# q and k of one chunk of tokens by seven block products instead of eight, and the gate's logits as two columns of v's products

## The chip, the cores and the metric

The kernel runs on one core of one Trainium2 chip. The time is the device time in microseconds, here the median of 3 timed runs; beside it stands one profiled execution, from which all rows below come. TensorE multiplies matrices and accumulates in PSUM (8 banks of 128 partitions x 512 float32), VectorE, ScalarE and GpSimd work element by element, and SyncE issues the DMAs.

## The reference

```python
x = A_x                                     # 2048 tokens x 448
g = sigmoid((x * gate_w).sum(-1))           # one gate per token
qkv = x @ wqkv                              # 16 heads of 28
logits = q . k over 8 past positions, 2 apart, * 28**-0.5
o = softmax(logits) . v                     # the same 8 positions
a = o @ wo
h = relu(x @ w1 + b1) ** 2                  # 1792 wide
b = h @ w2 + b2
out = g * a + (1 - g) * b
```

All products are wanted in float32 accuracy.

## The kernel before, in words

Tokens come in four chunks of 512 (chunk c holds four tiles of 128 tokens). Each float32 operand is split into a high part, rounded to the TensorE type (`fp32r`), and a low part, the rest; a product is made of three passes, high by high, high by low and low by high. ScalarE makes the high part (a copy), VectorE the low part (a subtraction): `split_full`. The 448 rows over which q, k and v are summed are three whole row tiles of 128 and a last one of 64. So that 64 rows do not take the time of 128, nearly all products are made of 64 rows at a time, two of them side by side in the two halves of the array (`side_by_side`), into two different banks; when the halves of a bank's sum change sides, a small VectorE write to the bank (`turn`) orders the one after the other.

`qkv_first` makes q, k and v of the first chunk (36 whole products of 128 rows, then pairs), `qkv_two` those of the others, two token tiles at a time. `qkv_evacuate` copies a finished bank to a stage tile with ScalarE; SyncE stores stage tiles to q_d, k_d and v_d in DRAM, from which attention (GpSimd multiplies, VectorE reduces) loads them again with its neighbours. Attention's first loads are issued when the second chunk's stores are, and wait for them.

The gate's logits are computed by VectorE from the raw chunk (`z_product`, `z_sums`), stored, loaded in another order and summed (`z_store`, `z_load`, `z_last`).

The program is written by one pass over TensorE's work that keeps a clock of its own (`advance`); `when(t, ...)` puts a step of another engine at a time of that clock, which sets only the place in each engine's queue, in which it then waits for its data. Steps of that kind are the splits of each chunk's x (`SPLIT_AT`), the spilling of x to DRAM for the MLP, and the four quarters of w1 (`w1_piece(i, t, gap)`: the load where it is called, the splits from t on). Raw loads of x, w1 and w2 share two buffers (`rawp`).

After the four chunks come the MLP (banks h, then b) and the products with wo (banks a), in an order written out by hand.

Of the kernel before, what the change touches and what calls it, by code (L numbers as in the profile page):

```python
# [14 lines left out]
P = 128  # L15
# [8 lines left out]
NQ = D + 2  # L24
NZ = 64
NP = 512
# [31 lines left out]
def gated_mix_kernel(ctx: ExitStack, tc: tile.TileContext, xT, wqkv, w1, w2, wo, b1, b2, out):  # L58
# [11 lines left out]
    z_d = tc.dram_tile([P, NZ], F32, name="z_d")  # L70
# [10 lines left out]
    w1h = const.tile([P, 3, F], F32R, name="w1h")  # L81
    w1l = const.tile([P, 3, F], F32R, name="w1l")
# [8 lines left out]

    xpool = ctx.enter_context(tc.tile_pool(name="xpool", bufs=1))
# [5 lines left out]
    zg = smallp.tile([P, 6, NS], F32, name="zg")  # L98
    zt, gt, g1t = zg[:, 0:2], zg[:, 2:4], zg[:, 4:6]
# [54 lines left out]
    wqh = ap.tile([P, 3, NP + 2 * D], F32R, name="wqh")  # L154
    wql = ap.tile([P, 3, NP + 2 * D], F32R, name="wql")

    w7h = ap.tile([P, NP + D], F32R, name="w7h")
    w7l = ap.tile([P, NP + D], F32R, name="w7l")
# [3 lines left out]
    nc.gpsimd.memset(halo0, 0.0)  # L162

    stage = {}

    def block(b):

        o = (0, NP, NP + D)[b]
        return slice(o, o + D)
# [29 lines left out]
    def qkv_evacuate(pt, c, tl, b):  # L199
        par, t = c // 2, (c % 2) * 4 + tl  # L200
        first = (b, t // 2) not in stage
        if first:
            stage[b, t // 2] = xap.tile([P, G, 2, C], F32, tag="stage", name=f"st{c}_{tl}_{b}", bufs=ST_BUFS)
        st = stage[b, t // 2]
        nc.scalar.activation(st[:, :, t % 2], pt[:, :D].rearrange("p (g c) -> p g c", g=G), AF.Copy)  # L205
        if not first:
            stage.pop((b, t // 2))
            t0 = t - t % 2
            dst, off = ((q_d, 0), (k_d, HALO), (v_d, HALO))[b]
            dd = dst[par, :, off:off + SP].rearrange("g (p s) c -> p g s c", s=NS)[:, :, t0:t0 + 2]  # L210
            nc.sync.dma_start(dd.rearrange("p g s c -> p g (s c)"), st.rearrange("p g s c -> p g (s c)"))
# [9 lines left out]
    def last(x, acc, tl, b):  # L221

        sl = slice(tl * P, tl * P + P)
        n = block(1) if b == 2 else slice(0, D)
        h, l = w7h[:, n], w7l[:, n]
        return [(acc, x.x7[:, sl], h), (acc, x.x7[:, sl], l), (acc, x.x8[:, sl], h)]

    def accs(c, b, tls, tags):
        return [Acc(t, f"qkv{c}_{tl}_{b}", D) for t, tl in zip(tags, tls)]
# [60 lines left out]


# [101 lines left out]
    def gates(par):  # L393

        e = smp.tile([P, 32], F32, tag="e", name=f"e{par}")[:, :NS]
        nc.scalar.activation(e, zt[:, par], AF.Exp, scale=-1.0)
# [127 lines left out]
    def w1_piece(i, dt, gap):  # L524
# [4 lines left out]
        sl = slice(i * n, (i + 1) * n)  # L529

        def part(k):
            if k < 3 and i > 1:
                split_copied(dt + k * gap, raw[:, k, :n], [(slice(0, P), slice(0, n), w1h[:, k, sl], w1l[:, k, sl])])
                return
            if k < 3:
                split_full(raw[:, k, :n], w1h[:, k, sl], w1l[:, k, sl], soon)
                return
# [47 lines left out]
    def h_full(x, acc, f, ks):  # L585
        fs = slice(f * P, f * P + P)
        return sum((three(acc, w1h[:, k, fs], w1l[:, k, fs], x.h[k], x.l[k]) for k in ks), [])
# [11 lines left out]
    def h_turn(accs, f):  # L599
        touch(w1h[:, 2].rearrange("p (f n) -> p f n", n=P)[:, f:f + 2, 0:1])  # L600
        for a in accs:
            a.rows = None
# [34 lines left out]
    raws = [raw_tile("wqraw0")]  # L637
    rx = raw_tile("xraw0")
    for k in range(4):
        if k < 3:  # L640
            nc.sync.dma_start(raws[0][:, k, :NQ], wqkv[0, :, k])
        else:
            for b, rows in ((0, slice(0, 64)), (1, slice(64, P))):
                nc.sync.dma_start(raws[0][rows, k, :NQ], wqkv[b, rows, k])
# [3 lines left out]
    for b, tag in ((1, "k"), (2, "v")):  # L648
        raw = attp.tile([P, 3, D], F32, tag=tag, name=f"wqraw{b}")
        for k in range(3):  # L650
            nc.sync.dma_start(raw[:, k], wqkv[b, :, k, :D])
        raws.append(raw)
    raw7 = attp.tile([P, D], F32, tag="q", name="wqraw7")
    nc.sync.dma_start(raw7, wqkv[2, :, 3, :D])
    x = x_tiles(0, xap)
    for k in range(3):
        nc.scalar.activation(wqh[:, k, :D], raws[0][:, k, :D], AF.Copy)
# [7 lines left out]
        nc.vector.tensor_sub(wql[:, k, :D], raws[0][:, k, :D], f32(wqh[:, k, :D]))  # L665
        for cols in halves:
            nc.vector.tensor_sub(x.l[k][:, cols], rx[:, k, cols], f32(x.h[k][:, cols]))
    split_full(raws[0][:, 3, :D], w7h[:, :D], w7l[:, :D])
    split_x78(rx[:, 3], x.x7, x.x8)

    zs = smp.tile([P, 3, NZ], F32, tag="lg", name="zs")
    zu = xcp.tile([P, CH], F32, tag="zu", name="zu")
    zpart, zall, gw = zs[:, 0], zs[:, 1], zs[:, 2, 0:4]
    nc.vector.tensor_copy(gw, raws[0][:, :, D])

    def z_product(raw, k):

        r = slice(0, P if k < 3 else 64)
        if k:
            nc.vector.scalar_tensor_tensor(zu[r], raw[r, k], gw[r, k:k + 1], zu[r], op0=ALU.mult, op1=ALU.add)  # L680
        else:
            nc.vector.tensor_scalar_mul(zu, raw[:, 0], gw[:, 0:1])

    def z_sums(c):

        nc.vector.transpose(zu, zu)
        nc.vector.tensor_reduce(
            zpart.rearrange("p (b c t) -> p c t b", b=4, c=4)[:, c],
            zu.rearrange("p (t b r) -> p t b r", t=4, b=4), axis=AX.X, op=ALU.add)

    def z_store():

        nc.sync.dma_start(z_d, zpart)

    def z_load():

        for b in range(4):
            nc.sync.dma_start(
                zall[b * 32:b * 32 + 32].rearrange("p (a n) -> p a n", a=4),
                z_d[:, b * 16:b * 16 + 16].rearrange("(a c) n -> c a n", a=4))  # L700

    def z_last():

        nc.vector.tensor_reduce(
            zt.rearrange("p q s -> p (q s)"), zall.rearrange("p (a n) -> p n a", a=4), axis=AX.X, op=ALU.add)

    def wq_split(b, k):
        if k < 3:
            split_full(raws[b][:, k], wqh[:, k, block(b)], wql[:, k, block(b)])
        else:  # L710
            split_full(raw7, w7h[:, NP:], w7l[:, NP:])
# [8 lines left out]
    SPLIT_AT = {1: 19000.0, 2: 35000.0, 3: 53500.0}  # L720

    def x_begin(c):
# [6 lines left out]
        if c == 1:  # L729
            xs[c] = X(own, [prodp.tile([P, W * C], F32R, tag="pp", name=f"x{c}_3{n}", bufs=PP_BUFS)[:, 48:48 + CH]  # L730
                            for n in range(2)])
            return
        xm[c] = x_tiles(c, xpool)
        xs[c] = X(own + xm[c].t[3:])
        for j in range(3):
            at(12000.0 + j * 2000.0, lambda j=j: nc.scalar.activation(xm[c].t[j], f32(own[j]), AF.Copy))
# [16 lines left out]
    for k in range(4):  # L753
        when(15000.0 + k * 700.0, z_product, rx, k)
    when(17900.0, z_sums, 0)
    when(60500.0, z_store)
    when(76000.0, z_load)
    when(86500.0, z_last)
    for c, t in SPLIT_AT.items():
        when(t, x_begin, c)  # L760
        for k in range(4):
            when(t + k * 900.0, lambda c, k: x_split(xraw[c], xs[c], k), c, k)
            when(t + k * 900.0 + 450.0, lambda c, k: z_product(xraw[c], k), c, k)
        when(t + 4200.0, z_sums, c)
# [456 lines left out]
```

## Time and profile before

| what | value |
|---|---|
| timed runs, median (lowest to highest) | 413.44 us (413.13 to 413.84) |
| profiled execution, first to last instruction | 412.0 us |
| TensorE busy | 407.8 us (99%) |
| VectorE, ScalarE, GpSimd busy | 270.6, 210.4, 268.4 us |
| DMA, mean over the span | 73.83 MB, 179 GB/s |

The profiled execution is given by its span; the timed runs' median lies 1.4 us above it, for what comes before the first and after the last instruction. Rows of the trace give start and duration in us, engine, line, operation, destination<-sources and shape; in brackets stands how long the engine had been idle and what ended that. "64*128" is a product of 64 rows in one half of the array, "128*128" one of all 128 rows. PEld is the loading of weights, which runs beside the products.

### The profile page before, as it was taken

How to read it: one execution, taken by the hardware profiler on the slowest of the kernel's cores; microseconds unless marked ns; L12 is line 12 of the kernel's file. 1: busy time of each engine (PE TensorE's matmuls, PEld its weight loads, DVE VectorE, ACT ScalarE, POOL GpSimd, SP SyncE). 2: the span in 40 equal slices, each digit the busy share in tenths (PEclk: the TensorE clock that was granted, in tenths of full speed). 3: DMA queues.
4: the chain of work that ended last, by engine and by line, in shares of the span. 5: the costliest groups of instructions: out<-in, count | busy, mean ns of one | idle time of the engine just before them, and what ended most of it. 6: DMA issues, size and time to landing. Idle time of an engine off the chain costs nothing.

```text
span 412.0 us, 9331 instructions
## 1 busy us (share of the span) xinstructions
PE 407.8 (99%) x3835; PEld 366.0 (89%) x3835; DVE 270.6 (66%) x430; ACT 210.4 (51%) x461; POOL 268.4 (65%) x167
## 2 busy tenths in 40 slices
PE   8999999999999999999999999999999999999997
PEld 7999999999888888888888888989898888888996
DVE  4590745276767766787656798879576677892354
ACT  4641646387775555444565535444653254346540
POOL 0000001955999999989989899999899977940000
PEclk9999999999999999999999999999999999999999
DMA  7999999979262315654112649765146530168304
GB/s 213 368 351 309 286 390 288 355 223 315 91 241 99 128 51 209 208 186 152 41 47 105 222 158 270 196 146 154 28 157 200 217 130 2 45 179 132 95 0 181
DMA packets 66763, 73.83 MB, mean 179 GB/s; under 512 B 33120, under 2 KB 59296, under 8 KB 66464
## 3 DMA queue, kind: packets, MB, share of 16 engines
q1 hardware_dynamic: 66720, 73.23, 55.4%
q8 instruction: 30, 0.49, 0.5%
q14 instruction: 13, 0.11, 0.1%
HBM read 45.74 MB, written 28.28 MB: 180 GB/s over the span
## 4 chain that ended last, share of the span: by engine, by line
PE 99%; DVE 0%; issue 0%
PE b L186 33%; PE h L186 32%; PE qkv L186 23%; PE a L186 7%; PE qkv L255 2%; PE warm L634 1%; PE a L993 1%; PE last L993 0%; DVE bt L872 0%; PE last L985 0%; PE a L985 0%; DVE zero L631 0%; DVE b1z L632 0%
## 5 line engine op out<-in xcount | busy, mean ns | idle before, releaser
L335 POOL TENSOR_TENSOR qk<-q,k 128x896 f32<-128x896 f32 x64 | 135.2, 2144 | 84.2 <-DMA k<-k_d 76.0
L342 POOL TENSOR_TENSOR av<-lg,v 128x896 f32<-128x896 f32 x64 | 119.2, 1957 | 6.2 <-DVE lg L336 5.6
L621 DVE TENSOR_TENSOR h<-h,h 128x512 fp32r<-128x512 f32 x56 | 38.4, 688 | 66.8 <-ACT h L624 66.5
L186 PE MATMUL qkv<-wqh,x 64*128 64x448 f32 x528 | 78.2, 359 | 0.0
L336 DVE TENSOR_REDUCE lg<-qk 128x32 f32<-128x896 f32 x64 | 67.0, 1074 | 0.0
L350 DVE TENSOR_REDUCE o<-av 128x112 f32<-128x896 f32 x64 | 66.4, 1070 | 0.1
L186 PE MATMUL b<-w2ah,h 64*128 64x448 f32 x448 | 66.3, 359 | 0.0
L186 PE MATMUL b<-w2bh,h 64*128 64x448 f32 x448 | 66.1, 359 | 0.0
L622 ACT ACTIVATE h<-h,b1z 128x512 f32<-128x512 f32 x56 | 36.7, 655 | 43.6 <-PE h L186 43.6
L186 PEld LDWEIGHTS qkv<-wqh,x 64*128 64x128 f32 x528 | 49.4, 184 | 3.6
L186 PE MATMUL qkv<-wql,x 64*128 64x448 f32 x264 | 47.7, 358 | 0.0
L186 PEld LDWEIGHTS b<-w2bh,h 64*128 64x128 f32 x448 | 42.1, 184 | 3.5
L186 PEld LDWEIGHTS b<-w2ah,h 64*128 64x128 f32 x448 | 42.0, 184 | 3.7
L205 ACT ACTIVATE st<-qkv 128x448 f32<-128x448 f32 x48 | 23.5, 542 | 34.3 <-PE qkv L186 31.7
L186 PE MATMUL b<-w2bl,h 64*128 64x448 f32 x224 | 40.7, 358 | 0.0
L186 PE MATMUL b<-w2al,h 64*128 64x448 f32 x224 | 40.5, 358 | 0.0
L623 ACT ACTIVATE h<-h 128x512 fp32r<-128x512 f32 x56 | 33.5, 598 | 1.7
L624 ACT ACTIVATE h<-h 128x512 f32<-128x512 f32 x56 | 33.3, 594 | 0.0
L573 ACT ACTIVATE h<-h 128x4 fp32r<-128x4 f32 (+1 forms) x35 | 7.2, 207 | 44.4 <-PE b L186 44.2
L186 PE MATMUL h<-x2b,w1h 64*128 64x512 f32 x168 | 28.1, 386 | 0.0
L186 PE MATMUL h<-x,w1h 64*128 64x512 f32 x168 | 28.1, 386 | 0.0
L186 PE MATMUL h<-x1b,w1h 64*128 64x512 f32 x168 | 28.1, 386 | 0.0
(150 smaller groups left out, 688.6 us busy)
## 6 DMA issues: line engine op xcount, KB each, us to landing
k<-k_d SPq DMA_DIRECT2D x8, 840.0 KB, 5.6
v<-v_d SPq DMA_DIRECT2D x8, 840.0 KB, 5.0
x_d<-x SPq DMA_DIRECT2D x11, 512.0 KB, 6.8
q_d<-st SPq DMA_DIRECT2D x8, 448.0 KB, 5.5
k_d<-st SPq DMA_DIRECT2D x8, 448.0 KB, 5.2
v_d<-st SPq DMA_DIRECT2D x8, 448.0 KB, 5.8
w1raw<-w SPq DMA_DIRECT2D x4, 896.0 KB, 9.2
q<-q_d SPq DMA_DIRECT2D x8, 448.0 KB, 3.6
```

The source lines that it names most:

```text
L186: nc.tensor.matmul(acc.pt[:, :acc.n], a[rows], w[rows], start=acc.todo == acc.all, stop=acc.todo == 1)
L205: nc.scalar.activation(st[:, :, t % 2], pt[:, :D].rearrange("p (g c) -> p g c", g=G), AF.Copy)
L255: nc.tensor.matmul(acc.pt[:, :D], a, w, start=k == j == 0, stop=False)
L335: nc.gpsimd.tensor_mul(pr, q[:, s:s + 1].to_broadcast([P, W, C]), k[:, s:s + W])
L336: pending.append(lambda: nc.vector.tensor_reduce(lg[:, s], pr.rearrange("p w (h d) -> p w h d", h=HG), axis=AX.X, op=ALU.add))
L342: nc.gpsimd.tensor_mul(pr.rearrange("p (h d) w -> p w h d", h=HG), lg[:, s][:, :, :, None].to_broadcast([P, W, HG, DH]), v[:, s:s + W].rea ...
L350: nc.vector.tensor_reduce(o[:, g * C:(g + 1) * C], pr, axis=AX.X, op=ALU.add)
L573: nc.scalar.activation(ap, f32(ap), AF.Copy)
L621: nc.vector.tensor_sub(hl, pt, f32(hh))
L622: ops += [lambda pt=pt, r=r: nc.scalar.activation(pt, pt, AF.Relu, bias=b1t[:, f + r:f + r + 1]), lambda pt=pt, hh=hh: nc.scalar.activatio ...
L623: lambda pt=pt, hh=hh: nc.scalar.activation(hh, pt, AF.Square),
L624: lambda pt=pt, r=r, low=low: (nc.scalar.activation(pt, pt, AF.Square), at(delays[r], low))]
```

## The change

Of the third chunk (c = 2), the four tiles are two groups of two. Within a group, two token tiles by two row tiles times two row tiles by two outputs (q and k) is a product of 2 by 2 blocks; it is made of seven block products of sums of blocks (Strassen's way, in Winograd's form) instead of eight. The row tiles 0 and 1 are one such product of whole tiles; the last tile of 64 rows with half of tile 2 is another, on half of the rows (`part`), the two groups side by side. The other half of tile 2 is done in the old way (`rest`). Sums of weights are made in the raw tiles and split (`weight_sums`, into the not yet used places of w2), sums of tokens in the raw chunk (`token_sums`). The seven products are added up in four banks per group, x, y, z and w: products 1, 6 and 7 in x, with a copy of x by ScalarE to a stage tile after each (`copied`), after which the next goes on adding; banks y, w, z and x are then added to the stage tiles by VectorE (`added`). v of this chunk comes first, by whole products (`v_tiles`).

The gate's weights are two more columns (450 instead of 448) of v's weights in all chunks, and ScalarE copies one of them with each v.

To fit, w1 is held in two halves, and steps move: x of the fourth chunk is loaded at 47500 of the clock instead of 39500, the second quarter of w1 at 54000 instead of 46500 with its splits from 60500 instead of 58500, and the copies of the fourth chunk's x for the MLP (`x_copies`) come after the third chunk.

```diff
     def block(b):
-        o = (0, NP, NP + D)[b]
-        return slice(o, o + D)
+        return slice(b * D, b * D + (NV if b == 2 else D))
...
+        if b == 2:
+            nc.scalar.activation(zt[par][:, t:t + 1], pt[:, D:D + 1], AF.Copy)
...
+    class Bank:
...
+            nc.tensor.matmul(self.pt[:, :self.n], a, w, start=new, stop=True, skip_group_check=True)
...
+    def whole(*todo):
+        for bank, prods in todo:
+            for a, w in prods:
+                bank.add(a, w)
+            advance(3 * MM448)
+
+    def halved(low, high):
+        for two in zip(low[1], high[1]):
+            for bank, (a, w) in zip((low[0], high[0]), two):
+                bank.add(a, w)
+        advance(3 * MM448)
...
+            one, two = (2, 3) if half else (0, 1)
+            return {1: lambda: (self.tokens(0, one), q(one)), 2: lambda: (self.tokens(0, two), q(two)),
+                    3: lambda: (self.token_sums(4, two), k(two)), 4: lambda: (self.tokens(1, two), wsum[4, half]),
+                    5: lambda: (self.token_sums(1, two), wsum[1, half]),
+                    6: lambda: (self.token_sums(2, one), wsum[2, half]),
+                    7: lambda: (self.token_sums(3, one), wsum[3, half])}[n]()
...
+            name = {1: "x", 2: "y", 3: "z", 4: "w", 5: "z", 6: "x", 7: "x"}[n]
...
+        def copied(self, n, b, r):
+            nc.scalar.activation(self.stage(b)[:, :, r], heads(self.to(n).pt), AF.Copy)
+
+        def added(self, n, b, r, store=False):
+            st = self.stage(b)
+            nc.vector.tensor_add(st[:, :, r], heads(self.to(n).pt), st[:, :, r])
...
+        parts(1)
+        parts(2)
+        turned(2)
+        wholes(1)
+        each("copied", 1, 0, 0)
+        wholes(2)
+        other(2, 0, 0)
+        each("added", 2, 0, 0)
+        parts(5)
+        wholes(5)
+        each("copied", 5, 1, 1)
+        parts(4)
+        turned(4)
+        parts(6)
+        wholes(6)
+        each("copied", 6, 1, 0)
+        wholes(4)
+        other(4, 1, 0)
+        other(3, 0, 1)
+        turned(3)
+        parts(7)
+        wholes(7)
+        each("copied", 7, 0, 1)
+        each("added", 4, 0, 1, True)
+        wholes(3)
+        parts(3)
+        each("added", 3, 1, 0)
+        other(7, 1, 1)
+        each("added", 7, 1, 1, True)
+
+    def v_tiles(c, x, tls, inner):
+        two = [(Bank(f"v{c}_{tl}", "b", NV), tl) for tl in tls]
...
+        for bank, tl in two:
+            whole(*((bank, ops(tl, j)) for j in range(3)))
+        halved(*((bank, [(a[rows], w[rows]) for a, w in ops(tl, 3)]) for (bank, tl), rows in zip(two, (LOW, HIGH))))
+        for bank, tl in two:
+            qkv_evacuate(bank.pt, c, tl, 2, inner)
...
+    nc.sync.dma_start(raw7[:, 0], wqkv[2, :, 3])
+    for b, rows in ((1, slice(0, 64)), (0, slice(64, P))):
+        nc.sync.dma_start(raw7[rows, 1, :D], wqkv[b, rows, 3, :D])
...
-    SPLIT_AT = {1: 19000.0, 2: 35000.0, 3: 53500.0}
+    SPLIT_AT = {1: 19000.0, 2: 35000.0, 3: 55000.0}
...
-    when(17900.0, z_sums, 0)
-    when(60500.0, z_store)
-    when(76000.0, z_load)
-    when(86500.0, z_last)
+    steps(24000.0, 900.0, weight_sums())
...
-            when(t + 4500.0, x_more, c + 1)
...
+    when(23500.0, x_more, 2)
+    when(47500.0, x_more, 3)
+    when(46900.0, lambda: steps(47000.0, 900.0, token_sums(2)))
...
-    when(46500.0, w1_piece, 1, 58500.0, 1500.0)
-    when(67000.0, w1_piece, 2, 77400.0, 1450.0)
...
+    when(54000.0, w1_piece, 1, 60500.0, 1500.0)
+    when(66000.0, w1_piece, 2, 75600.0, 1450.0)
...
+    v_tiles(2, xs[2], (0, 1), True)
+    v_tiles(2, xs[2], (2, 3), True)
+    qk_seven(2, xs[2])
+    x_copies(3)
```

In SyncE's queue, around the end of the second chunk, before (w1raw_795 is the second quarter of w1; st, the stage tiles of the second chunk's last q, k and v; q, k and v, attention's first loads):

```order
L528 DMA w1raw_795<-w 128x4x448 [waits DMAHW0_49,DVE_49]
L211 DMA q_d<-st_2_0_809 128x4x224 [waits DMAHW1_49,Activation_49]
L211 DMA k_d<-st_3_1_811 128x4x224 [waits DMAHW2_49,Activation_49]
L211 DMA v_d<-st_2_2_853 128x4x224 [waits DMAHW3_49,Activation_49]
L306 DMA q_857<-q_d 128x896 [waits DMAHW4_49,DMAHW1_49]
L307 DMA k_858<-k_d 128x1680 [waits DMAHW6_49,DMAHW5_49,DMAHW2_49]
L312 DMA v_861<-v_d 128x1680 [waits DMAHW7_49,DMAHW3_49]
```

The same place now (xraw_833 is x of the fourth chunk, w1raw_927 the second quarter of w1):

```order
L772 DMA xraw_833<-xT 128x2048 [waits DMAHW0_49,DVE_49]
L225 DMA q_d<-st_2_0_835 128x4x224 [waits DMAHW1_49,Activation_49]
L225 DMA k_d<-st_3_1_837 128x4x224 [waits DMAHW2_49,Activation_49]
L225 DMA v_d<-st_2_2_892 128x4x224 [waits DMAHW3_49,Activation_49]
L507 DMA q_898<-q_d 128x896 [waits DMAHW4_49,DMAHW1_49]
L508 DMA k_899<-k_d 128x1680 [waits DMAHW6_49,DMAHW5_49,DMAHW2_49]
L513 DMA v_902<-v_d 128x1680 [waits DMAHW7_49,DMAHW3_49]
L729 DMA w1raw_927<-w 128x4x448 [waits DVE_49]
```

The quarter's load has moved from ahead of the stores to behind the loads that wait for them.

In ScalarE's queue, the splits of that quarter before, between the splits of the fourth chunk's x and the copies of the third chunk's first q and k:

```order
L115 ACTIVATE x_3_923<-xraw_738 128x512
L115 ACTIVATE w1h<-w1raw_795 128x448 [waits DMAHW0_49]
L115 ACTIVATE w1h<-w1raw_795 128x448
L205 ACTIVATE st_0_0_988<-qkv_0_0_863 128x4x112 [waits DVE_49,DMAHW1_49,PE_49,Activation_49]
L205 ACTIVATE st_1_1_990<-qkv_1_1_866 128x4x112 [waits DMAHW2_49,DVE_49,Activation_49]
```

And now, between the copies of v's last gate column (e_131) and of the two groups' product 1 out of banks x:

```order
L235 ACTIVATE e_131<-v_3_964 128x1
L129 ACTIVATE w1ah<-w1raw_927 128x448 [waits DMAHW7_49]
L129 ACTIVATE w1ah<-w1raw_927 128x448
L423 ACTIVATE st_0_0_1014<-x_0_988 128x4x112 [waits DMAHW1_49,PE_49,Activation_49]
L423 ACTIVATE st_1_0_1016<-x_1_990 128x4x112 [waits DMAHW2_49,PE_49,Activation_49]
```

In both, two splits of the quarter stand ahead of copies out of the third chunk's banks; what has changed is which banks these are, and who uses them next.

On TensorE, a piece of the third chunk's first pair of tiles before; all of it is made of pairs of 64 rows, into banks that take turns:

```order
L186 MATMUL qkv_0_0_863<-w7h,x_3_636 128x448
L186 MATMUL qkv_1_1_866<-w7h,x_3_636 128x448
L186 MATMUL qkv_1_0_864<-wqh,x_0_633 128x448 [waits Activation_49]
L186 MATMUL qkv_0_1_865<-wqh,x_0_633 128x448 [waits Activation_49]
L186 MATMUL qkv_1_0_864<-wql,x_0_633 128x448
```

And now, in the middle of the seven products: the last whole products 5 (banks z), the halves of product 4 (banks w) and the first halves of product 6 (banks x, with product 1 in them):

```order
L334 MATMUL z_1_1037<-w2ah,s_1h 128x448
L334 MATMUL z_1_1037<-w2al,s_1h 128x448
L334 MATMUL z_1_1037<-w2ah,s_1l 128x448
L334 MATMUL w_0_1058<-tw_208,x_3_653 128x448 [waits PE_49,Activation_49]
L334 MATMUL w_1_1060<-tw_208,x_3_653 128x448 [waits PE_49,Activation_49]
L334 MATMUL w_0_1058<-tw_208,x_3_653 128x448
L334 MATMUL w_1_1060<-tw_208,x_3_653 128x448
L334 MATMUL w_0_1058<-tw_208,x_3_653 128x448
L334 MATMUL w_1_1060<-tw_208,x_3_653 128x448
L334 MATMUL x_0_988<-w2ah,s_0h 128x448 [waits Activation_49]
L334 MATMUL x_1_990<-w2ah,s_0h 128x448 [waits Activation_49]
```

The rows of z are products of 128 rows, one after the other into one bank; those of w and x are pairs of 64 rows. The two waits at x are for ScalarE's copies of product 1.

More of the change, by code (lines that the diff above doesn't have):

```diff
@@ L23 @@
 CH = 512
-NQ = D + 2
-NZ = 64
-NP = 512
+NV = D + 2
+NB = 512
 SCALE = float(DH) ** -0.5
@@ new lines, in whole, with weights @@
+    def whole(*todo):
[8 more added lines that the diff above has]
+        advance(3 * MM448)
+    def weights(b, j):
+        if j < 3:
+            return wqh[:, j, block(b)], wql[:, j, block(b)]
+        return w7h[:, D:D + NV], w7l[:, D:D + NV]
@@ L585, in h_full @@
     def h_full(x, acc, f, ks):
-        fs = slice(f * P, f * P + P)
-        return sum((three(acc, w1h[:, k, fs], w1l[:, k, fs], x.h[k], x.l[k]) for k in ks), [])
+        return sum((three(acc, w1_f(0, k, f), w1_f(1, k, f), x.h[k], x.l[k]) for k in ks), [])
     def h_last(x, acc, f):
```

292 lines of the change are left out of this document (202 added, 90 removed).

## The prediction

> **What bounds the kernel now.** I read the page first (busy times, chain), then TensorE's waits, then its busy time by stage.
>
> ```profile
> span 412.0 us, 9331 instructions
> PE 407.8 (99%) x3835; PEld 366.0 (89%) x3835; DVE 270.6 (66%) x430; ACT 210.4 (51%) x461; POOL 268.4 (65%) x167
> PE 99%; DVE 0%; issue 0%
> PE warm L634 <- DVE b1z L632: 1.2, 1, 1.2
> ```
>
> TensorE is busy 99% of the span, the chain that ends last is TensorE alone, and its only wait is 1.2 us before the warm-up. So a product removed is time gained, and every new wait of TensorE is time lost: there is no slack in which to hide one.
>
> ```profile
> 31.30:56.50 25.20, 25.20 (x256) 23.52 (x254) 9.40 (x29) 10.17 (x23) 0.00 (x0) 1.00 0.97 320
> 56.50:81.70 25.20, 25.20 (x256) 23.52 (x254) 11.60 (x31) 13.49 (x26) 10.81 (x6) 1.00 0.98 334
> 56.71 0.98 ACT L205 ACTIVATE st<-qkv 128x448 f32<-128x448 f32 x2 [0.87 <-ACT st L205]
> 81.91 0.98 ACT L205 ACTIVATE st<-qkv 128x448 f32<-128x448 f32 x2 [0.87 <-ACT st L205]
> ```
>
> The two windows are the second and third chunk; the two ScalarE rows are the copies of their last v, which start as TensorE ends them, 25.20 us apart. A chunk has 4 token tiles x 3 outputs x 3.5 row tiles x 3 passes = 126 slots (a slot is one product of 128 rows, or two of 64 rows side by side), so a slot takes 25.20 / 126 = 0.200 us. The windows also show VectorE and ScalarE about half busy or less (11.60 and 13.49 of 25.20), and in their last three columns the granted clock full (1.00), the DMA engines full (0.97 and 0.98) and what they moved (320 and 334 GB/s): a load that moves back in the queue lands later by as much.
>
> **Products.** q and k of the third chunk took 84 slots. Seven products of whole tiles make 2 groups x 7 x 3 = 42, their halves 7 x 3 = 21, the other 64 rows 4 x 3 = 12: 75 slots. Nine fewer at 0.200 are -1.80 us. The gate's logits widen each v product by two columns:
>
> ```profile
> 116.73 2.40 PE b L186 x24
> 119.13 2.72 PE h L186 x24
> ```
>
> Twelve slots of 448 columns take 2.40, of 512 columns 2.72: 0.0267 us for 64 columns, 0.00083 for two, and 168 v slots make +0.14. The dot products on VectorE that they replace lay beside TensorE and give nothing.
>
> **Changes between 64-row and 128-row products.** Until now all products but the first 36 and the last 18 stand in pairs of 64 rows. So the trace has two such changes.
>
> ```profile
> 12.65 0.56 PE L255 MATMUL qkv<-wqh,x 128*128 128x448 f32 x2
> 13.14 0.47 PE L186 MATMUL qkv<-w7h,x 64*128 64x448 f32 x2
> 13.45 0.37 PE L186 MATMUL qkv<-w7l,x 64*128 64x448 f32 x2
> 13.65 0.57 PE L186 MATMUL qkv<-w7h,x 64*128 64x448 f32 x4
> 13.14 0.19 PEld L186 LDWEIGHTS qkv<-w7h,x 64*128 64x128 f32 x2 [0.30 <-ACT wqh L115]
> 404.52 0.45 PE L186 MATMUL b<-w2bl,h 64*128 64x448 f32 x2
> 404.90 0.47 PE L993 MATMUL a<-woh,o 128*128 128x448 f32 x1
> 405.21 0.37 PE L993 MATMUL a<-wol,o 128*128 128x448 f32 x1
> 405.41 0.57 PE L993 MATMUL a<-woh,o 128*128 128x448 f32 x2
> 404.90 0.19 PEld L993 LDWEIGHTS a<-woh,o 128*128 128x128 f32 x1 [0.30 <-issue]
> ```
>
> From 12.65 to 13.45 three slots pass (two whole products, one pair): 0.80 instead of 0.60. From 404.52 to 405.21 two slots take 0.69 instead of 0.40, of which 0.09 may belong to the uneven pairs before. At both places the weight load, elsewhere hidden, sits idle 0.30. I take 0.20 for one change, bounds 0 (if both gaps waited for something else, as the label on the first says) and 0.29. After 405.21 whole products into one bank follow each other every 0.20, so those cost no more. The new code changes form 4 times in v and 8 times in the seven products: 12 x 0.20 = +2.40.
>
> The Trainium skill says, in "TensorEngine Tiling (Array Packing)", section "Key Properties", that a change of the tiling mode, not of the tile alone, drains TensorE. It gives no time. By it each of the twelve costs something, and the bound of 0 falls away; both gaps above agree.
>
> **The quarter of w1 behind attention's loads.** The second quarter's load (`w1_piece(1)`) moves in SyncE's queue from before the stores of the second chunk to behind attention's first loads, which wait for those stores.
>
> ```profile
> 52.49 0.59 SPq L528 DMA_DIRECT2D w1raw<-w  x1
> 55.43 0.38 SPq L211 DMA_DIRECT2D q_d<-st  x1
> 63.16 0.33 SPq L306 DMA_DIRECT2D q<-q_d  x1
> 64.51 0.34 SPq L307 DMA_DIRECT2D k<-k_d  x1
> 65.85 0.32 SPq L312 DMA_DIRECT2D v<-v_d  x1
> k<-k_d SPq DMA_DIRECT2D x8, 840.0 KB, 5.6
> v<-v_d SPq DMA_DIRECT2D x8, 840.0 KB, 5.0
> w1raw<-w SPq DMA_DIRECT2D x4, 896.0 KB, 9.2
> q<-q_d SPq DMA_DIRECT2D x8, 448.0 KB, 3.6
> DMA to landing us min/median/max: 6.4/9.2/9.7
> 61.87 1.05 ACT L115 ACTIVATE w1h<-w1raw 128x448 fp32r<-128x448 f32 x2 [1.96 <-DMA w1raw<-w]
> ```
>
> The load left at 52.49, its split on ScalarE waited 1.96 us for it and began at 61.87, and behind it stood nothing that TensorE needed soon. Now it leaves after the load of v, which left at 65.85. Ahead of the stores there are 0.92 MB less (the quarter) and 0.23 more (the second copy of the last row tile): 0.69 MB at 334 GB/s is 2.1 us, so the load of v leaves at 63.8 and the quarter at 64.1. By the median of the four quarters, 9.2 (the row of minimum, median and maximum is theirs), it lands at 73.3; by bytes, 448 + 840 + 840 + 896 KB = 3.10 MB at 334 GB/s from 63.8 on, at 73.1. I take 73.3. Bounds: 70.5 (64.1 + 6.4) and 75.9 (no store lands earlier, 66.2 + 9.7).
>
> On ScalarE the first two splits of the quarter (1.05, the row at 61.87) now stand ahead of the copies of product 1 out of banks x (0.98 for two, the rows at 56.71), and product 6, which goes on adding in these banks, waits for the copies: 73.3 + 0.1 + 1.05 + 0.98 = 75.4.
>
> When does TensorE ask? The second chunk ends at 56.5, and 0.22 later now (84 v slots x 0.00083, and 0.15 for a turn, below). v: 42 x 0.201 = 8.43. Then 33 slots up to product 6's halves: 6.60. Eight changes of form: 1.60. Together 73.35. So TensorE waits 75.4 - 73.35 = +2.05; with the bounds of the landing 0 and 4.65. The term shares its time with the changes ahead of it: were they free, TensorE would ask at 71.75 and wait 3.65.
>
> **Small waits at turns and at the chunk's end.** Rows for VectorE:
>
> ```profile
> L336 DVE TENSOR_REDUCE lg<-qk 128x32 f32<-128x896 f32 x64 | 67.0, 1074 | 0.0
> L520 DVE TENSOR_TENSOR w2al<-copy,w2ah 128x448 fp32r<-128x448 f32 x7 | 4.4, 630 | 3.3 <-ACT copy L515 3.2
> 83.83 0.62 DVE L520 TENSOR_TENSOR w1l<-copy,w1h 128x448 fp32r<-128x448 f32 x1 [5.06 <-ACT copy L515]
> 90.44 0.06 DVE L196 MEMSET qkv<- 1x1 f32 x2
> ```
>
> The fourth chunk's first q takes the bank out of which VectorE adds product 3 to k. That add (nearest row, also out of PSUM: 0.63) begins after the last of product 3 and, in queue order, after a reduction of attention (1.07); meanwhile TensorE has three slots of its own, 0.60. With 0.2 from engine to engine and some rest of the reduction I take +0.5, bounds 0.2 and 1.3.
>
> In the fourth chunk the second turn stood at 90.44. Pairs begin at 81.7, and slot 45 needs it at 81.7 + 9.0 = 90.7: a margin of 0.26. Now three adds (1.9) and another reduction (1.07) come first, less some 2.1 that VectorE idled at the start of that stretch for ScalarE (its first work there was at 83.83 against 81.7). That is 0.6 over the margin; with three copies of x now on ScalarE in between I take +0.7, bounds 0 and 1.6.
>
> In the second chunk the sums of weights add 22 operations on VectorE and 11 on ScalarE, some 0.6 each, to engines 9.40 and 10.17 busy of 25.20. They fit, but the splits of x and w1 queue behind them, and one turn comes about 0.15 late; bounds 0 and 0.6. The sums of tokens end on VectorE before the third chunk's v is done.
>
> **Sum.** -1.80 + 0.14 + 2.40 + 2.05 + 0.5 + 0.7 + 0.15 = +4.1 us: span 416.1. The timed median, 413.44, lies 1.4 above the profiled span of 412.0; with the same 1.4, 417.5. All waits at their low ends, with changes of form at 0.20, give -1.66 + 2.40 + 0.2 = +0.9; all at their high ends -1.66 + 2.40 + 4.65 + 1.3 + 1.6 + 0.6 = +8.9, but hardly all together.
>
> **Rivals.**
>
> 1. The quarter lands in time. The DMA engines serve 16 rings side by side, and the 6.4 us of the fastest quarter would bring it at 70.5; ScalarE is through at 72.6, before 73.35. Then the sum is +2.1: 415.5. Against it: DMA share 0.98 in that window, and 3.10 MB that must pass.
>
> 2. Faster: changes of form are free. Both gaps were waits of another kind (the label "ACT wqh" on the first, "issue" on the second). Then 2.40 goes. Whether it ends faster is decided by the landing: TensorE asks at 71.75, and every 0.1 us after 69.7 (71.75 less the 2.1 us of ScalarE's work) costs 0.1. With the landing by then the rest is -1.66 + 0.2 to 1.3, so -0.9 at 412.5 and at best 412.0; at the landing of 73.3 the same rival gives +3.4 and 416.8, hardly other than my forecast. For it speaks only that there are just two such places.
>
> 3. Slower still: a wait of two to four microseconds in mid-stream lets the clock fall, or VectorE, now late, holds up more turns in the fourth chunk.
>
> ```profile
> 4.22 1.09 PE L255 MATMUL qkv<-wqh,x 128*128 128x448 f32 x2
> 5.11 0.95 PE L255 MATMUL qkv<-wql,x 128*128 128x448 f32 x2
> 5.86 1.59 PE L255 MATMUL qkv<-wqh,x 128*128 128x448 f32 x4
> ```
>
> At the start, four products took from 4.22 to 5.86, 1.64 instead of 0.80. The Trainium skill puts the fall of the clock, in "TensorE: Matmul & The Clock Gate", section "What's actually happening", at an idle window of some 3.4 us; no trace here shows one in mid-stream. Such a start repeated after the wait adds 0.84; with every small wait at its high end 2.1 more: 418.3 to 420.5.
>
> **How the numbers follow.** Forecast (late landing; 415.9 to 419.6, centre 417.5): 0.65. Rival 1 (414.5 to 416.3): 0.17. Rival 2 with an early landing (412.0 to 413.5): 0.09. Rival 3: 0.09. A measurement of this kernel can tell about 0.2%, 0.83 us, from no change. Faster by more needs rival 2 at its best: 0.06. Within 0.2%: the rest of rival 2 and the lowest of rival 1: 0.07. Slower: 0.87. The range from 414.2 to 419.8 holds the forecast, nearly all of rival 1 and half of rival 3.
>
> **What would show it.** Right: TensorE's waits name a ScalarE copy out of x (line 423), 1 to 4 us long, near 73 us; ahead of it on ScalarE a split of w1raw ended by its DMA near 73; the first product after each change of form comes 0.29 after the last; the fourth chunk begins near 85 with a wait for VectorE's add (line 427). Wrong: no wait at line 334 in that stretch (rival 1, if the whole products still start 0.3 late; rival 2, if they follow at 0.20), or the lost time lying after 115 us.

## The result, and the profile after

The changed kernel takes 429.97 us (median of 4 runs, 429.42 to 430.18) against 413.39 (413.13 to 413.84): 1.0395 times as long, 95% interval 1.0378 to 1.0412. The direction was foretold; the size (417.5, range 414.2 to 419.8) was not. The profiled execution took 430.18 us, its span 428.4.

From the page after, the span, the busy times and the chain that ended last; then TensorE's longest waits (us in total, times, longest; the 1.2 of the warm-up, the same as before, is left out):

```profile
span 428.4 us, 9182 instructions
PE 413.9 (97%) x3739; PEld 388.9 (91%) x3739; DVE 280.8 (66%) x438; ACT 219.9 (51%) x498; POOL 267.9 (63%) x167
PE 81%; DVE 5%; DMA 5%; ACT 4%; POOL 1%; issue 1%; SPq 0%; DVEq 0%; ACTq 0%; POOLq 0%
PE qkv L201 <- DVE qkv L211: 3.4, 3, 1.5
PE h L201 <- ACT w1ah L778: 3.1, 1, 3.1
PE h L201 <- ACT st L233: 1.9, 1, 1.9
PE x L334 <- ACT st L423: 1.0, 1, 1.0
```

Where TensorE was 99% of the chain, it is now 81%: VectorE, DMA, ScalarE and GpSimd have come onto the path. Only the last of these four waits is the one foretold. The timeline of TensorE tells in which stage the loss lies (start, busy us, and in brackets the idle time before the row and what ended it). First before, the first product of the MLP's first half and the first of its second half; then after, the begin of the fourth chunk, its two late turns, and the same places:

```profile
104.60 0.40 PE L186 MATMUL h<-x,w17h 64*128 64x512 f32 x2
116.57 0.36 PE L186 MATMUL b<-w2ah,h 64*128 64x448 f32 x2
```

```profile
75.28 0.90 PE L334 MATMUL x<-w2ah,s_0h 64*128 64x448 f32 x2 [1.00 <-ACT st L423]
85.82 0.47 PE L201 MATMUL qkv<-wqh,x 64*128 64x448 f32 x2 [0.21 <-DVE st L427]
94.89 0.47 PE L201 MATMUL qkv<-wqh,x 64*128 64x448 f32 x2 [1.53 <-DVE qkv L211]
98.29 0.48 PE L201 MATMUL qkv<-wqh,x 64*128 64x448 f32 x2 [1.31 <-DVE qkv L211]
112.28 0.40 PE L201 MATMUL h<-x,w17h 64*128 64x512 f32 x2
119.52 0.50 PE L201 MATMUL h<-x,w1ah 64*128 64x512 f32 x2 [3.09 <-ACT w1ah L778]
123.97 0.50 PE L201 MATMUL h<-x,w17h 64*128 64x512 f32 x1 [1.87 <-ACT st L233]
131.48 0.36 PE L201 MATMUL b<-w2ah,h 64*128 64x448 f32 x1
```

The fourth chunk begins 4.16 us later than before (85.82 against 81.66, where its first product starts in the kernel before). From there to the first h it takes 26.46 instead of 22.94, 3.52 more; from the first h to the first b 19.20 instead of 11.97, 7.23 more. What follows adds 1.5, and the sum is the span's 16.4. So the part that the prediction worked out in detail came out at +4.16 instead of +3.4, and the other twelve microseconds lie behind it.

**The late turns.** VectorE's timeline after:

```profile
92.15 0.62 DVE L721 TENSOR_TENSOR w1bl<-copy,w1bh 128x448 fp32r<-128x448 f32 x1 [3.27 <-DMA k_d<-st]
94.75 0.06 DVE L211 MEMSET qkv<- 1x1 f32 x2
98.15 0.64 DVE L211 MEMSET qkv<- 1x1 f32 x4
```

The low part of w1's second half is written into the tile with the tag `e4`, and in that tile `Group.stage` had put k of the second pair of token tiles. So VectorE must wait for k's store to land, 3.27 us, with the turns that TensorE needs behind it.

**The two waits near 120.** SyncE's queue, first before, then after, and then the engines that wait in turn:

```profile
88.26 0.39 SPq L556 DMA_DIRECT2D w2raw<-w  x1
90.46 0.34 SPq L306 DMA_DIRECT2D q<-q_d  x1
90.85 0.42 SPq L307 DMA_DIRECT2D k<-k_d  x1
95.69 0.37 SPq L211 DMA_DIRECT2D q_d<-st  x1
```

```profile
96.02 0.37 SPq L761 DMA_DIRECT2D w2raw<-w  x1
103.77 0.36 SPq L225 DMA_DIRECT2D q_d<-st  x1
104.22 0.46 SPq L225 DMA_DIRECT2D k_d<-st  x1
104.73 0.90 SPq L761 DMA_DIRECT2D w2raw<-w  x1
105.72 1.22 SPq L507 DMA_DIRECT2D q<-q_d  x1
106.99 0.48 SPq L508 DMA_DIRECT2D k<-k_d  x1
115.01 6.22 POOL L536 TENSOR_TENSOR qk<-q,k 128x896 f32<-128x896 f32 x3 [17.00 <-DMA k<-k_d]
117.14 1.09 DVE L537 TENSOR_REDUCE lg<-qk 128x32 f32<-128x896 f32 x1 [6.02 <-POOL qk L536]
118.80 0.55 ACT L716 ACTIVATE copy<-w2raw 128x448 f32<-128x448 f32 x1 [5.08 <-DVE w2al L721]
122.91 0.55 ACT L716 ACTIVATE copy<-w2raw 128x448 f32<-128x448 f32 x1 [2.97 <-DVE w2al L721]
```

Before, attention's second loads of q and k stood ahead of the fourth chunk's stores. Now they stand behind two of them, which wait for copies that ScalarE makes near 103, and behind the load of the second piece of w2. So q and k leave 15 to 16 us later and GpSimd stands still for 17.00 us. VectorE waits for GpSimd at its next reduction, ScalarE at its copy of w2 for VectorE's low part behind that reduction, and behind ScalarE's copies stand the two instructions for which TensorE waits 3.09 and 1.87 us.

**The clock.** Three windows after (the third number from the right is the granted clock):

```profile
124.00:126.00 2.00, 2.00 (x14) 1.62 (x16) 1.65 (x4) 1.97 (x5) 2.00 (x2) 0.74 0.57 187
126.00:128.00 2.00, 2.00 (x12) 1.57 (x10) 2.00 (x3) 0.99 (x3) 2.00 (x2) 0.50 0.83 272
128.00:130.00 2.00, 2.00 (x20) 1.88 (x18) 0.72 (x3) 1.34 (x4) 2.00 (x2) 0.91 0.00 0
```

The missing shares, 0.26, 0.50 and 0.09 of 2 us each, make 1.7 us: half clock for some 3.4 us. With the idle 3.09 + 1.87 these are 6.7 of the 7.23 in this profiled run.

### The profile page after: what moved, and what is told of

Read it like the earlier page. It is cut to its first block, busy times and chain, and to the rows that moved or that the text cites. A ratio compares the mean times of both kernels' runs of the same rounds, so it can differ in the third digit from the quotient of the medians.

```text
span 428.4 us, 9182 instructions
## 1 busy us (share of the span) xinstructions
PE 413.9 (97%) x3739; PEld 388.9 (91%) x3739; DVE 280.8 (66%) x438; ACT 219.9 (51%) x498; POOL 267.9 (63%) x167
## 4 chain that ended last, share of the span: by engine, by line
PE 81%; DVE 5%; DMA 5%; ACT 4%; POOL 1%; issue 1%; SPq 0%; DVEq 0%; ACTq 0%; POOLq 0%
PE h L201 30%; PE b L201 30%; PE qkv L201 8%; PE a L201 7%; DMA w1raw<-w 2%; PE qkv L281 2%; DMA k<-k_d 2%; POOL qk L536 1%; PE v L334 1%; DMA k_d<-st 1%; ACT st L233 1%; ACT copy L716 1%; DVE st L427 1%; DVE w1al L130 1%; PE warm L843 1%
## 5 line engine op out<-in xcount | busy, mean ns | idle before, releaser
L201 PE MATMUL qkv<-wqh,x 64*128 64x448 f32 (+1 forms) x384 | 58.3, 363 | 3.6 <-DVE qkv L211 3.4
L201 PEld LDWEIGHTS b<-w2ah,h 64*128 64x128 f32 x448 | 56.5, 184 | 0.3
L201 PEld LDWEIGHTS b<-w2bh,h 64*128 64x128 f32 x448 | 52.8, 184 | 1.7 <-DVE h L830 0.8
L201 PE MATMUL b<-w2al,h 64*128 64x448 f32 x224 | 52.5, 358 | 0.0
L201 PE MATMUL b<-w2bl,h 64*128 64x448 f32 x224 | 49.6, 359 | 0.0
L201 PEld LDWEIGHTS qkv<-wqh,x 64*128 64x128 f32 x384 | 36.9, 185 | 7.8 <-DVE qkv L211 4.5
L201 PE MATMUL qkv<-wql,x 64*128 64x448 f32 (+1 forms) x192 | 35.4, 360 | 0.0
L201 PEld LDWEIGHTS b<-w2al,h 64*128 64x128 f32 x224 | 32.2, 184 | 0.1
L201 PEld LDWEIGHTS b<-w2bl,h 64*128 64x128 f32 x224 | 29.5, 184 | 0.4
L201 PE MATMUL h<-x,w1ah 64*128 64x512 f32 x84 | 19.5, 418 | 3.1 <-ACT w1ah L778 3.1
```

Of the source, the lines that this page charges most:

```text
L201: nc.tensor.matmul(acc.pt[:, :acc.n], a[rows], w[rows], start=acc.todo == acc.all, stop=acc.todo == 1)
```

## The experiments

Of each kernel's timeline the table gives the begin of the fourth chunk, the time from there to the first h, from there to the first b, and the timed median (us). All rows but the first contain the whole change, with the edits that are named; "both" is the ground on which those below it are built.

| kernel | 4th chunk begins | to first h | to first b | time |
|---|---|---|---|---|
| before | 81.66 | 22.94 | 11.97 | 413.4 |
| after | 85.82 | 26.46 | 19.20 | 430.0 |
| split order | 87.44 | 23.27 | 17.67 | 427.0 |
| stores later | 87.50 | 25.46 | 13.51 | 425.7 |
| both | 85.78 | 23.28 | 13.32 | 421.8 |
| quarter split later | 84.64 | 24.13 | 13.27 | 420.6 |
| v in pairs | 85.46 | 25.28 | 13.52 | 422.9 |
| six changes | 84.97 | 25.26 | 12.95 | 421.9 |
| quarter first | 83.40 | 23.29 | 13.33 | 418.8 |
| all | 85.33 | 24.60 | 12.18 | 422.4 |
| quarter first, six changes | 82.36 | 23.29 | 13.27 | 417.7 |

**Split order.** In `w1_piece`:

```diff
-        for k in range(4):
-            when(dt + k * gap, part, k)
+        for p, k in enumerate((0, 2, 3, 1) if i == 2 else range(4)):
+            when(dt + p * gap, part, k, p)
```

> Edit: of the third quarter of w1 the second row tile is split last (rows 0, 2, 3, 1 instead of 0, 1, 2, 3), so that VectorE's low part of it, which is written where the k of the second pair of token tiles was staged, comes some 4.4 us later in the queue than the end of that k's store. Theory A (two separate losses: this stop of VectorE costs the two turns in the fourth chunk, and attention's second loads behind the fourth chunk's stores in SyncE's queue cost the two waits near 120): the turns' 3.4 us go, the waits near 120 stay, 426.5 us. Rival B (one loss: VectorE, stopped at 88.8, is late for everything that follows, and GpSimd and the waits near 120 are late because of it): both go, 3.4 and 7.2 us, 419.4 us.

Measured 427.01, 1.0336 times before (1.0320 to 1.0352). Both late turns are gone (23.27 to the first h, 3.19 less than after), the long wait of the MLP is not:

```profile
118.04 0.80 PE L201 MATMUL h<-x,w1ah 64*128 64x512 f32 x2 [3.18 <-ACT w1ah L778]
```

So rival B falls: with that stop of VectorE gone, GpSimd is still late (its wait for k is 16.66 us instead of 17.00). The time falls by 3.0: 3.19 in the stretch of the turns and 1.53 in the MLP, whose two waits add up to 3.72 instead of 4.96, less 1.62 by which the third chunk ends later here; that is taken up below.

**Stores later.** In `qkv_evacuate` (and the second piece of w2 at 90000):

```diff
+            if c == 3 and tl < 2 and b < 2:
+                at(4000.0, lambda: stage_store(st, par, t - t % 2, b))
```

> Edit: the two stores of the fourth chunk's first q and k, and the load of the second piece of w2, are issued behind attention's second loads of q and k instead of ahead of them; nothing else moves. Theory A: the loads leave at about 98, when GpSimd has read the first q and k, instead of 105.7; GpSimd goes on near 107 instead of 115; the two waits of TensorE near 120 and the low clock behind them go (7.2 us), the two late turns stay: 422.8 us. Rival B: VectorE is as late as before, nearly nothing is won: 429 to 430 us. Against both: the delayed stores now hold ScalarE or the loads behind them, and a new wait of 1 to 2 us appears.

Measured 425.74 (423.61 to 426.58). Attention's loads leave at 98.70 and 99.09, the waits of the MLP shrink from 4.96 to 0.86 and the clock there stays full: 13.51 to the first b instead of 19.20, 5.7 less. The turns stay late (25.46). That is theory A; the time fell short of its 422.8 because here the third chunk lost more. Its wait at product 6 was 1.69 instead of 1.00, and after it the clock fell:

```profile
76.00:78.00 2.00, 2.00 (x10) 1.44 (x10) 2.00 (x4) 1.90 (x7) 2.00 (x2) 0.93 0.67 247
78.00:80.00 2.00, 2.00 (x7) 1.66 (x7) 1.95 (x4) 1.61 (x4) 2.00 (x1) 0.50 0.10 32
80.00:82.00 2.00, 2.00 (x12) 1.38 (x12) 1.37 (x4) 0.00 (x0) 0.42 (x1) 0.72 0.00 0
```

Again 3.4 us at half. The same happened in the kernel with the split order (wait 1.28), not in the changed kernel (1.00) nor with both edits (0.64): the fourth chunks of the two with the low clock begin at 87.5 and 87.4, those of the other two at 85.8, though the code up to there is the same.

**Both.**

> Both edits together (the split order and the stores behind the loads). Theory A and rival B alike: both losses go, 430.0 - 3.4 - 7.2 = 419.4 us, so the two orders are told apart by the single edits only. What is left over that the prediction did not have would be 1.3 us after 360 us.

Measured 421.80 (420.65 to 423.65): 8.2 of the expected 10.6 us. The two losses add up, as the table's row shows. The time is 2.4 over the expectation, and the runs lie 3 us apart. Their spans go with the mean granted clock: 418.9 and 419.3 at 0.999 and 1.000, 420.8 and 421.9 at 0.996. The profiled one is that of 419.3. In the kernel with the stores later they do not (its longest span, 424.8, had 1.000), so what spreads the runs is not shown.

**Quarter split later.** `when(54000.0, w1_piece, 1, 64000.0, 1500.0)` instead of 60500, on top of both.

> On top of both edits (split order, stores behind loads): the second quarter of w1 is split later in ScalarE's queue (model time 64000 instead of 60500), so that the copies of product 1 stand ahead of its splits and no longer wait for its load. Theory: TensorE's wait at product 6 (0.6 to 1.7 us in the four profiles so far) goes, and with it the low clock that followed where it was 1.3 us or longer: 419.5 us, with runs closer together than the 420.65 to 423.65 of the kernel with both edits. Rival: the load is late for whatever copy stands behind the splits; then the wait moves to the products into z or w and the time stays at 421 to 422 us.

Measured 420.56 (419.49 to 420.77). The wait at product 6 is gone, 1.1 us earlier at the fourth chunk, but two waits for turns came in its place:

```profile
81.64 0.47 PE L338 MATMUL z<-wqh,s_1h 128*128 128x448 f32 x1 [0.65 <-DVE z L450]
94.72 0.47 PE L201 MATMUL qkv<-wqh,x 64*128 64x448 f32 x2 [0.72 <-DVE qkv L211]
78.54 2.98 DVE L130 TENSOR_TENSOR w17l<-w1raw,w17h 64x64 fp32r<-64x64 f32 x4
```

The third row is what stood ahead of the turn of z on VectorE: four low parts of the quarter's last row tile. They took 2.98 us. Before, ahead of attention's first product, the same four took 1.29; the difference comes up again below:

```profile
68.75 1.29 DVE L116 TENSOR_TENSOR w17l<-w1raw,w17h 64x64 fp32r<-64x64 f32 x4 [0.94 <-ACT w17h L115]
```

**v in pairs**, and then **six changes**, each on top of the one ahead. The first replaces `v_tiles` by the order of the first chunk's v (pairs of 64 rows, four banks); the second reorders `qk_seven`:

```diff
-    v_tiles(2, xs[2], (0, 1), True)
-    v_tiles(2, xs[2], (2, 3), True)
+    v_pairs(2, xs[2])
...
         parts(2)
+        parts(5)
         turned(2)
         wholes(1)
         each("copied", 1, 0, 0)
         wholes(2)
-        other(2, 0, 0)
-        each("added", 2, 0, 0)
-        parts(5)
         wholes(5)
         each("copied", 5, 1, 1)
+        other(2, 0, 0)
+        each("added", 2, 0, 0)
         parts(4)
```

> On top of that, v of the third chunk in pairs of 64 rows throughout, as in the first chunk: the same 42 slots, but four changes between 64-row and 128-row products fewer. Theory (0.20 us for one change): 0.8 us less, 418.7 us, and the fourth chunk begins 0.8 us earlier. Rival (the late starts at these places are waits of another kind): the same time as the kernel without this edit.

> On top of that, the halves and the wholes of the seven products in another order: products 1, 2 and 5 halves first, then their wholes, so that six changes of form are left instead of eight (of twelve in the changed kernel). Theory: another 0.4 us less, 418.3 us; the seven products with their six changes would be worth 1.80 - 1.20 = 0.6 us, less the gate's 0.14. Rival: product 6 now follows product 1 sooner (18 slots instead of 21) and waits for ScalarE's copy of it: up to 1 us more.

Measured 422.94 and 421.93, slower than without them by 2.4 and 1.4; neither the theories nor the rivals had that. TensorE came sooner to turns that VectorE did not have ready. In the first of the two:

```profile
76.40 0.47 PE L338 MATMUL w<-w2ah,x 128*128 128x448 f32 x1 [0.96 <-DVE w L450]
82.46 0.47 PE L338 MATMUL z<-wqh,s_1h 128*128 128x448 f32 x1 [1.15 <-DVE z L450]
96.71 0.47 PE L201 MATMUL qkv<-wqh,x 64*128 64x448 f32 x2 [1.89 <-DVE qkv L211]
```

In the time, these waits hide what a change of form costs; a later kernel without them shows it.

**Quarter first.** `when(50500.0, w1_piece, 1, 60500.0, 1500.0)` on top of both, without the later split: the load stands ahead of attention's first loads.

> On top of the split order and the stores behind the loads: the second quarter of w1 is loaded ahead of attention's first loads again (one place ahead of the last v store of the second chunk). Its tile is free at about 61.3, so it leaves then and not at 64.0, and lands near 70.5 instead of 73.5. Theory: ScalarE splits it before TensorE asks for product 6 (73.4); that wait goes (0.6 us in the profile of the kernel with both edits, up to 1.7 elsewhere) and no low clock follows. VectorE's low parts of the quarter then mostly run before GpSimd begins on attention, which itself begins 2 to 3 us later: 420.6 us, 1.2 less than with both edits. Rival: attention's later start is paid back in the fourth chunk, where VectorE would wait for GpSimd: 422 us or more.

Measured 418.82 (418.56 to 419.12), 3.0 less than with both and 1.8 better than expected. The quarter left at 61.13 and ScalarE split it from 67.48. TensorE has no wait within the third chunk, the fourth begins at 83.40, and the runs lie 0.6 us apart instead of 3.

**All**: six changes, quarter first, its last row tile split later (72000), and q instead of k in the tile `e4`.

> The kernel with six changes of form, and: the quarter ahead of attention's first loads; the last row tile of the quarter split after the turns of banks w and z; of the second pair of token tiles q and not k is staged where a low part of w1's second half is written later (its store is 3 us earlier). Theory: the three waits left for VectorE's turns in the kernel with six changes (0.7 and 1.7 in the third chunk, 1.9 in the fourth) were (a) low parts of the quarter drawn out by GpSimd's products beside them and (b) the store of k again; all three go with 0.1 each for the new start: 421.9 - 4.6 = 417.3 us. What is left against the kernel before is then -1.80 + 0.14 + 6 x 0.20 and about 4 us of small waits. Rival: VectorE is late for its mere load; then one or two of the waits stay and the time is 419 to 421 us.

Measured 422.38 (420.64 to 423.42). The turns were in time, but I had put the quarter's last low parts ahead of VectorE's add of product 3, for which the fourth chunk's first bank waits, and TensorE waited 3.13 us for it, with 3.4 us of half clock behind:

```profile
81.84 2.90 DVE L130 TENSOR_TENSOR w17l<-w1raw,w17h 64x64 fp32r<-64x64 f32 x4
85.33 0.74 PE L201 MATMUL qkv<-wqh,x 64*128 64x448 f32 x2 [3.13 <-DVE st L431]
```

Neither the theory nor the rival meant this wait; it is of my own making.

**Quarter first and six changes**, without the two other edits.

> The kernel with the quarter ahead of attention's first loads (418.8 us, no wait in its third chunk), and in it v in pairs of 64 rows and the seven products in the order with six changes of form: six changes instead of twelve, nothing else; the last row tile of the quarter stays where that kernel split it, ahead of the adds. This asks again, without the turns that hid it, what a change of form costs. Theory (0.20 us each): 6 x 0.20 = 1.2 us less, 417.6 us, the fourth chunk beginning at 82.2 instead of 83.4. Rival: the third chunk ends sooner than VectorE's adds, and the bank of product 3 comes as late as before: the time gained turns into a wait for the add, 418.8 us.

Measured 417.69 (417.50 to 418.08), 1.0109 times before (1.0092 to 1.0126): 1.13 less for six changes of form. The fourth chunk begins 1.04 earlier. It is the fastest kernel here that has the seven products; none beat the kernel before.

**The gate alone.** `qk_seven`, `v_tiles` and the sums left out, third chunk by `qkv_two`; first with the quarter where the change has it, then with the load and split times of before.

> One part of the change alone: q and k of the third chunk by eight products as before, no sums of weights and tokens; the gate's logits in v's products and the tiles of the changed kernel stay, the times of the w1 and w2 splits are those of the kernel before (the second quarter of w1 stays behind attention's first loads). Theory A: all loss comes from the seven products and what their order does to VectorE, ScalarE and SyncE; the gate's columns cost 0.14 us: 413.5 us. Rival C: the moved quarter and the new tiles (stage tiles that share memory with the weights' halves) cost by themselves, 1 to 3 us: 414.5 to 416.5 us.

> The gate's logits in v's products alone, without the seven products, and now with the second quarter of w1, the x of the fourth chunk and all splits at the times of the kernel before (the first such kernel had the quarter behind attention's first loads and waited 4.9 us for it). Theory: the gate costs its two columns, 0.14 us: 413.5 us, and the 9.8 us of the first such kernel were the moved quarter, its wait and the low clock behind it. Rival: the gate's columns or the smaller stage tiles cost by themselves: 415 us or more.

Measured 423.15 and 415.72. Each has one long wait:

```profile
76.88 0.74 PE L201 MATMUL qkv<-wqh,x 64*128 64x448 f32 x1 [4.86 <-ACT st L233]
```

```profile
91.75 0.47 PE L201 MATMUL qkv<-wqh,x 64*128 64x448 f32 x2 [1.06 <-DVE qkv L211]
```

In the first, ScalarE's split of the quarter waits for its load until 75.36 and stands ahead of the copies that TensorE waits for. So without the seven products, the moved quarter costs most of the 7.4 us between the two kernels, which differ also in when the fourth chunk's x is loaded and split: 4.86 are the wait, and from its end to 81.69 the clock is at half, 4.81 us or 2.4 lost. Rival C (1 to 3 us) was right in kind and too low by far: this kernel is 9.8 over the one before.

In the second, the gate's columns themselves cost little. Of its 2.6 us, 1.33 are the fourth chunk's second turn (1.06 idle, the rest a slow start). VectorE had waited 0.96 there for ScalarE's copy of w1, and ahead of that stand two copies of the fourth chunk's x (1.05 and 1.04), which this kernel still makes after the third chunk; the kernel before has none there. By the two profiled spans (413.7 and 412.0) that leaves 0.4 for all the rest, with the 0.14 of the columns; but the profiled execution of before was one of its longer ones (the median span of its runs beside this kernel is 411.4), so up to 1.1 stay unexplained. The rival's time (415 or more) came, but neither theory nor rival meant this turn.

## Why the prediction was wrong

**Right, by its steps.** The quarter was to leave at 64.1 and land at 73.3; it left at 64.01, and ScalarE's split of it, which waited for it, began at 73.76, ahead of the copies of product 1:

```profile
73.76 1.04 ACT L129 ACTIVATE w1ah<-w1raw 128x448 fp32r<-128x448 f32 x2 [5.79 <-DMA w1raw<-w]
74.71 0.96 ACT L423 ACTIVATE st<-x 128x448 f32<-128x448 f32 x2
```

Product 6 was to wait 2.05 us for these copies. It was idle for 1.00, began 1.17 late in all, and the products after it another 0.55 late: 1.7. A change of form was taken at 0.20. The trace after shows it at all twelve places: the first product in the new form begins 0.29 to 0.30 after the last, the next 0.31 to 0.32 after that, where 0.20 is usual for each. One of the places, from halves to wholes of product 5:

```profile
71.69 0.37 PE L334 MATMUL z<-w2ah,s_1l 64*128 64x448 f32 x2
71.99 0.47 PE L334 MATMUL z<-w2ah,s_1h 128*128 128x448 f32 x1
72.30 0.37 PE L334 MATMUL z<-w2al,s_1h 128*128 128x448 f32 x1
```

That is 0.20 to 0.22 each, 2.5 for the 2.40; taking six away gave 1.13 in time and 1.04 at the fourth chunk. The Trainium skill's statement on the drain at a change of tiling mode ("TensorEngine Tiling (Array Packing)", "Key Properties") agrees. The bank of product 3 was late by 0.21 idle, 0.48 with the slow start behind, for 0.5. Nine slots fewer stand.

**Mis-sized.** "One turn comes about 0.15 late" in the second chunk: it is 0.58 idle in the kernel after and 0.57 to 0.59 in all others with the sums. Start to start it costs 0.84 (the product begins 0.93 after the last, the next 0.31 after that), above its bounds of 0 and 0.6. One turn in the third chunk, that of w, came 0.4 late behind a low part of the quarter and had no term. That 4.16 came near the 3.4 is in part luck: these turns took 1.1 more, the wait at product 6 0.3 less.

**The step that failed first** is "for the second turn I take +0.7, bounds 0 and 1.6". The stretch lost 3.52. The working counted VectorE's operations ahead of the turn and took each at its busy time. It did not ask for each of them what its output tile had held: the low part into `e4` waited 3.27 us for a store that the change itself had put there. Only the split order was needed to take 3.19 of it away.

**The step that was missing** is worth more. The prediction followed SyncE's queue for the one load that the change moves on purpose. But the third chunk became nine slots shorter by the kernel's planning clock, while attention goes by times of its own on that clock, so attention's second loads fell behind the fourth chunk's stores. (In the kernel with the gate alone, whose third chunk keeps its length, they leave at 98.75 and stand ahead. The changed kernel with `clock["att"] = clock["pe"] - 1.0 - 9 * MM448`, attention planned nine slots earlier and nothing else, has them ahead of the stores again in its program; it was not run.) The order of SyncE's queue can be read before any run; I took what stands behind the fourth chunk's begin as harmless. In the profiled run it cost 4.96 us of waits and 1.7 of clock; moving three entries gave 5.7 back. The prediction's own sign of being wrong, time lost after 115 us, is what came.

**Rival 3** named the clock and the turns, at 0.84 and 2.1 us. The clock cost 1.7 in the MLP of the profiled run, and what held TensorE up most was not a turn but a chain over SyncE, GpSimd, VectorE and ScalarE.

Even with most of it mended the change loses: 417.7. By its stages it is 0.70 late at the fourth chunk, 1.05 at the first h, 2.35 at the first b and 3.7 at the end of the span (4.3 by the timed medians). Five waits of TensorE are left, 1.8 us idle (0.57 in the second chunk, 0.20 at the fourth, 0.31 twice in the MLP, 0.38 near 375). But a wait costs more than its idle time. The row of the first:

```profile
51.45 0.47 PE L201 MATMUL qkv<-wqh,x 64*128 64x448 f32 x2 [0.57 <-DVE qkv L211]
```

The product before it began at 50.52, the next begins at 51.76. So 0.93 and 0.31 pass instead of 0.20 each: 0.84 lost with 0.57 idle. Counted so, the five waits cost 3.1, a turn that comes late without idle time 0.16, and the six changes 1.2, against 1.66 gained: 2.8 of the 3.7. Where the other 0.9 went is open.

## What to carry to other kernels

A chunk that gets shorter shifts everything that is placed by another clock. Compare the whole order of every in-order queue, stores and loads of later stages included, not only what the change means to move. For each instruction ahead of one that the bound engine needs, ask what its output memory held last and who has yet to read it; a shared tile can make a compute engine wait for a DMA (3.27 us here). TensorE was at 99% here, and no order that was tried kept the saving of 1.8 us.

## What the runs showed that I had not expected

**Half clock after short waits.** The granted clock fell to 0.50 for 3.4 us or twice that during or after waits of 1.28, 1.69, 3.13, 3.18 and 4.86 us, and after 1.87 that followed 3.09. It stayed full after 1.00, after 3.09 until that second wait was over, after 1.53 and 1.31 with 2.1 us between them, and after 1.89 and 1.93 (v in pairs, six changes). So the length alone doesn't decide. The Trainium skill ("TensorE: Matmul & The Clock Gate", "What's actually happening") tells of a free-running window of about 3.4 us; the length of the low spells agrees, and that where a wait lies in the window matters would fit, but is not shown. That the window must be idle does not agree: 1.28 us was enough (split order, the clock fell 0.8 us after the wait).

A low spell of 3.4 us costs up to 1.7 us, and not always that. The changed kernel's three other runs had mean clocks of 0.986 to 0.992 against the profiled run's 0.996, by estimate 7 to 12 us at half instead of 3.4, and still spans of 427.6 to 428.2 against 428.4. No trace shows where their low spells lay.

**VectorE beside GpSimd.** A low part of 128 x 448 with both inputs in SBUF took 0.63 us alone, and two of them took 4.67 while GpSimd ran attention's products (six changes):

```profile
75.97 4.67 DVE L130 TENSOR_TENSOR w1al<-w1raw,w1ah 128x448 fp32r<-128x448 f32 x2 [0.65 <-ACT w1ah L129]
75.57 4.59 POOL L548 TENSOR_TENSOR qk<-q,k 128x896 f32<-128x896 f32 x2 [2.56 <-ACT st L427]
```

Each of the two low parts ended about 0.5 us after one of GpSimd's products did; the products took 2.12 and 2.50, where 2.14 is the mean in the kernel before. The low parts out of the copy in PSUM take 0.62 beside GpSimd as well (in the changed kernel the one at 94.69, with GpSimd busy from 93.84 on, took 0.64). By the Trainium skill ("SBUF — State Buffer", "Who interferes with whom") a VectorE instruction with two SBUF inputs contends with a GpSimd instruction that reads SBUF; these rows agree. The change had moved the quarter's splits, which read SBUF twice, into the time in which attention runs.
